# Four plain batches and two seven-product pairs instead of six and one, in a fused attention and FFN kernel

## The chip, the cores and the metric

The kernel runs on one core of a Trainium2 chip. The metric is the device time of one execution in microseconds (us), the median over runs. The core has five engines, each with its own instruction queue that is worked off in order: PE (TensorE, matmuls into eight PSUM banks), DVE (VectorE), ACT (ScalarE), POOL (GpSimd, which has no access to PSUM) and SP (SyncE, which here only issues transfers).

## What is computed

Eight batches; each has 12 heads of 448 positions by 64, so 768 columns. Sigmoid attention, then a mixing of positions by two small matrices, then a feed-forward network (FFN) of width 3072:

```python
scores = scale * np.matmul(q, k.transpose(0, 1, 3, 2)) - np.log(S)
attn = 1.0 / (1.0 + np.exp(-scores))
x = np.matmul(attn, v)            # (8, 12, 448, 64) -> (8, 448, 768)
u = x + (x.transpose(0, 2, 1) @ U @ V).transpose(0, 2, 1)
out = u + np.maximum(u @ w_ch1, 0.0) @ w_ch2
```

## The kernel before

**Numbers in two parts.** Most matmuls are done in 16 bit floats: a 32 bit tile x is scaled and split into a high part (`scaled`, or an ACT instruction) and a rest, x·s minus the high part (`rest`, L329 to L336), and a product takes three matmuls (high·high, high·rest, rest·high). The weights arrive as 64 bit words, are decoded once during batch 0 (`decode`) and are then kept in two parts in memory (`scratch`), from where each later batch fetches them (`fetch`).

**Attention** of a batch is worked through by six head pairs (`pair`). For batches 2 to 7 a head pair loads q, k, v, takes bounds of them on ACT, finds three scales (`scale_by_dma`: a store, a broadcast load and four small DVE instructions), splits q, k and v into one of two staging buffers (STG, POOL and DVE), runs two score operations on PE (each fills four PSUM banks at once), eight sigmoids on ACT, seven splits (POOL for the high part, DVE for the rest) and one value operation on PE. ACT copies its bank into one of six tiles (UB). `mix` then mixes positions, parks the batch's u in memory and, for batches of the plain FFN, splits u into two parts. The UB tiles can be written again when the park has landed.

**The plain FFN** of a batch (`ffn_in`, `ffn_out`) goes by six groups of 512 hidden columns: 4 chains of 18 matmuls in, 6 chains of 12 out, 864 matmuls a batch. After an in chain ACT reads the bank twice (L800, L801) and DVE or POOL makes the rest (L803); after an out chain DVE adds the bank to u.

**The seven-product FFN** takes two batches together: blocks of two by two (two batches, two halves) are multiplied with seven products instead of eight. A pair is 12 in quads (`in_quad`) and 12 out quads (`out_quad`), each 63 matmuls (`product`, L923), in the order iiiiooo iiiooo iiiooo iiooo; a quad takes four of the eight banks. The inputs of the pair are made by `u_forms` (loads of parked u, four subtractions and seven splits for each of three columns). The weights' side needs sums of weight quarters, in two parts: `quarter_sums` copies three quarters, adds and subtracts eight times on POOL and stores four sums through two output buffers (WO, one ACT and one DVE instruction and a store each). There are 24 of them (12 quarters by two weights), and before the change they all run beside attention, in batches 1 to 4 (`FORMS`). `factors` loads a quad's weights into one of four buffers. Tiles of a pair live in any free place of other buffers (`SPOT`; for the making of the inputs `EARLY`, the buffers of attention alone).

**What sets the order.** All operations are first listed with an engine, a planned cost, a position `pos` (a due time) and dependences. `Plan.order` then plays them through: at each moment it takes, among what could start, the operation with the lowest `pos`. The instructions of each engine are emitted in that order, which is fixed from then on. `BEGIN` holds the planned start of each plain batch; the FFN takes its `pos` from it, and attention is spread by a step d per head pair between `BEGIN[1]` and `BEGIN[PLAIN - 1]`. `PLAIN` is the number of plain batches, `LATER` the order in which batches 2 to 7 pass through attention. FFN uses banks `PF` (four), attention `PS_` (four).

## Time and profile before

| | |
|---|---|
| median of 3 runs | 1640.53 us (1640.19 to 1640.63) |
| profiled execution | 1642.12 us, its span 1640.0 us |
| PE, DVE, ACT, POOL busy | 1605.2, 1181.3, 736.5, 616.1 us |
| mean granted TensorE clock | 0.992 |
| moved by DMA | 302.31 MB, 184 GB/s on average |

A span goes from the first to the last instruction of the program; the time of the execution holds a little more around it. Busy times are the union of an engine's instructions. Instructions of one engine can overlap a little, so that the sum of their durations is larger than its busy time; matmuls overlap most, and their cost is read from the distance of their starts.

### The profile page before, as it was taken

What the parts mean: (1) busy time and instruction counts of PE and PEld (TensorE: products, weight loads), DVE (VectorE), ACT (ScalarE), POOL (GpSimd) and SP (SyncE); (2) the same over time, 40 slices, a digit from 0 to 9 for tenths busy, and PEclk for the clock granted to TensorE, in tenths of its full rate; (3) what the DMA queues carried; (4) which work ended last, traced back from release to release, by engine and by line L of the source; (5) the groups of instructions that cost most, each with busy time, mean ns of one, the idle gap of its engine ahead of it and who ended that gap; (6) DMA issues with size and microseconds to landing.
All of it is one profiled execution on the core that took longest, in us unless ns stands there. A gap on an engine that the chain in (4) does not pass through costs nothing.

```text
span 1640.0 us, 24443 instructions
## 1 busy us (share of the span) xinstructions
PE 1605.2 (98%) x8975; PEld 787.5 (48%) x8975; DVE 1181.3 (72%) x2024; ACT 736.5 (45%) x1408; POOL 616.1 (38%) x646
## 2 busy tenths in 40 slices
PE   8989999999999999999999999999999999999999
PEld 3334445544454444445444544544555555555554
DVE  2789999768888788876887787878552357564746
ACT  7566786364545453553555455344311233140310
POOL 0233344447728655843874495257400000000000
PEclk9989999999999999999999999999999999999999
DMA  8757875856666777667765677644783334232331
GB/s 234 256 199 246 310 258 206 285 161 182 198 175 189 209 186 217 167 199 198 228 177 157 199 204 220 173 139 131 185 290 132 119 127 173 104 133 101 118 119 68
DMA packets 203641, 302.31 MB, mean 184 GB/s; under 512 B 106497, under 2 KB 178817, under 8 KB 191233
## 3 DMA queue, kind: packets, MB, share of 16 engines
q1 hardware_dynamic: 203520, 300.75, 59.8%
q8 instruction: 70, 1.15, 0.3%
q14 instruction: 51, 0.41, 0.1%
HBM read 219.81 MB, written 72.60 MB: 178 GB/s over the span
## 4 chain that ended last, share of the span: by engine, by line
PE 73%; DVE 12%; DMA 5%; POOL 5%; issue 2%; ACT 2%; SPq 1%; ACTq 0%; POOLq 0%; DVEq 0%
PE bank L814 22%; PE bank L793 22%; PE bank L923 17%; PE bank L466 4%; PE bank L481 3%; DMA w<-w_in 2%; DVE us__88 L330 2%; POOL w L858 1%; DVE stg__124 L330 1%; PE bank L477 1%; DVE stg__125 L330 1%; POOL w L862 1%; SPq L311 1%; DMA row__136<-far 1%; DMA forms<-xn__121 1%
## 5 line engine op out<-in xcount | busy, mean ns | idle before, releaser
L814 PE MATMUL bank<-h__94,w__92 128*128 128x448 f16 x1296 | 261.6, 354 | 0.0
L814 PE MATMUL bank<-h__93,w__91 128*128 128x448 f16 x1296 | 258.6, 353 | 0.0
L793 PEld LDWEIGHTS <-w__89 128*128 128x128 f16 x1296 | 125.3, 98 | 126.3 <-issue 14.9
L793 PEld LDWEIGHTS <-w__90 128*128 128x128 f16 x1296 | 126.1, 98 | 122.9 <-issue 7.2
L814 PEld LDWEIGHTS <-w__91 128*128 128x128 f16 x1296 | 123.7, 98 | 124.6 <-issue 14.2
L814 PEld LDWEIGHTS <-w__92 128*128 128x128 f16 x1296 | 124.6, 99 | 122.8 <-issue 13.8
L793 PE MATMUL bank<-us__87,w__89 128*128 128x448 f16 x864 | 170.6, 353 | 2.4 <-DVE inv_w__206 L351 1.0
L793 PE MATMUL bank<-us__87,w__90 128*128 128x448 f16 x864 | 172.5, 355 | 0.3 <-POOL w__90 L762 0.3
L862 POOL TENSOR_TENSOR w<-w 128x384 f32<-128x384 f32 x96 | 110.8, 1154 | 3.8
L800 ACT ACTIVATE r__96<-bank 128x448 f32<-128x448 f32 x71 | 38.2, 538 | 146.2 <-PE bank L793 146.2
L800 ACT ACTIVATE r__95<-bank 128x448 f32<-128x448 f32 x73 | 39.4, 540 | 115.5 <-PE bank L793 114.5
L793 PE MATMUL bank<-us__88,w__89 128*128 128x448 f16 x432 | 87.1, 356 | 0.0
L793 PE MATMUL bank<-us__88,w__90 128*128 128x448 f16 x432 | 85.7, 353 | 0.0
L550 ACT ACTIVATE a<-bank,bias_s,c__240 128x448 f32<-128x448 f32 (+1 forms) x96 | 65.6, 723 | 28.7 <-PE bank L466 16.0
L550 ACT ACTIVATE a<-bank,bias_s,c__239 128x448 f32<-128x448 f32 (+1 forms) x96 | 65.8, 723 | 24.7 <-PE bank L466 12.3
L550 ACT ACTIVATE a<-bank,bias_s,c__241 128x448 f32<-128x448 f32 (+1 forms) x96 | 65.4, 721 | 20.2 <-PE bank L466 10.2
L923 PEld LDWEIGHTS <-w__89 128*128 128x128 f16 x441 | 43.1, 98 | 40.3
L803 DVE TENSOR_TENSOR h__94<-r__95,h__94 128x448 f16<-128x448 f32 x36 | 28.6, 796 | 36.0 <-ACT h__94 L801 35.8
L923 PEld LDWEIGHTS <-w__90 128*128 128x128 f16 x378 | 37.0, 98 | 34.5
L923 PEld LDWEIGHTS <-w__91 128*128 128x128 f16 x378 | 37.0, 98 | 34.5
L466 PE MATMUL bank<-stg__124 64*128 64x448 f16 x432 | 48.4, 351 | 2.2 <-ACT a L550 1.9
L466 PE MATMUL bank<-stg__125 64*128 64x448 f16 x432 | 47.7, 351 | 0.2 <-ACT ub__83 L586 0.2
(1164 smaller groups left out, 3263.9 us busy)
## 6 DMA issues: line engine op xcount, KB each, us to landing
w<-w_in SPq DMA_DIRECT2D x48, 768.0 KB, 5.9
w__89<-scratch SPq DMA_DIRECT2D x15, 1536.0 KB, 8.2
w__90<-scratch SPq DMA_DIRECT2D x15, 1536.0 KB, 7.9
w__91<-scratch SPq DMA_DIRECT2D x15, 1536.0 KB, 8.5
w__92<-scratch SPq DMA_DIRECT2D x15, 1536.0 KB, 8.2
w__89<-forms SPq DMA_DIRECT2D x7, 1344.0 KB, 5.7
forms<-xn__120 SPq DMA_DIRECT2D x48, 192.0 KB, 2.9
forms<-xn__121 SPq DMA_DIRECT2D x48, 192.0 KB, 3.3
```

Of the source, the lines that this page charges most:

```text
L311: op("SP", max(0.6, n / 0.30e6), lambda: nc.sync.dma_start(out=dst(), in_=src()), reads, writes, pos, land=land)
L330: nc.vector.scalar_tensor_tensor(out=out, in0=in0, scalar=s, in1=in1, op0=op0, op1=op1)
L466: nc.tensor.matmul(o, keys, y[rows_of(h)], start=i == 0, stop=i == n - 1)
L477: nc.tensor.matmul(av.x[:, :S], x[:, 3, :], y(tiles[3, 0]), start=i == 0, stop=False, skip_group_check=True)
L481: nc.tensor.matmul(av.x[rows_of(h), :S], x[:, j, rows_of(h)], y(tiles[j, h]), start=False, stop=j == 2 and i == n - 1, skip_group_check=True,)
L550: act(0.65 if whole else 0.73, lambda: nc.scalar.activation(out_(), in_(), AF.Sigmoid, bias=bias_s[rows], scale=c if whole else c.x[rows]) ...
L793: nc.tensor.matmul(ph.x[:, :S], wx[:, x, c, f * P : (f + 1) * P], us.x[:, c, y, :], start=c == 0 and i == 0, stop=c == NP - 1 and i == 2,)
L800: act(0.54, lambda: nc.scalar.activation(r.x, ph.x[:, :S], AF.Relu, scale=DOWN_H), [ph], [r], pos - 4)
L803: (pool if on_pool else dve)(1.25 if on_pool else 0.71, lambda: (nc.gpsimd if on_pool else nc.vector).tensor_tensor(out=h.x[:, f, 1, :], i ...
L814: nc.tensor.matmul(po.x[:, :S], wx[:, x, f, e * P : (e + 1) * P], h.x[:, f, y, :], start=f == 0 and i == 0, stop=f == FC - 1 and i == 2,)
L862: pool(0.9, lambda o_=o_, x=x, y=y, sub=sub: nc.gpsimd.tensor_tensor(out=t.x[:, o_], in0=t.x[:, x], in1=t.x[:, y], op=ALU.subtract if sub ...
L923: nc.tensor.matmul(bank.x[:, :S], wt.x[:, k, FACTOR[n], x], both(f)[:, y], start=start and k == i == 0, stop=k == 2 and i == 2, skip_group ...
```

## The change

`PLAIN` falls from 6 to 4, so batches 4 and 5 join 6 and 7 as a second seven-product pair, which runs first. Attention for batches 2 to 7 is now spread to 60 planned us before the end of the last plain batch. From batch 1 on FFN has three banks, and from batch 2 on attention has five. Only weight groups 0 and 1 have their sums made beside plain batches 1 and 2; the other 16 quarter sums read the weights from `scratch` into a buffer of their own (`WSRC`) and stand beside the first pair, which in turn has fewer places for its tiles (`MID`). `u_forms` scales u in place on ACT first, makes its subtractions and two of seven rests on POOL, and for the second pair waits for the last product but seven listed so far (`begun[-8]`, the last of the eleventh in quad). In `scale_by_dma` and `pair` four small DVE instructions become three on POOL. Several planned costs are changed as well.

```diff
-PLAIN = 6
-LATER = [2, 3, 6, 4, 5, 7]
-FORMS = {1: (3,), 2: (1, 4), 3: (2,), 4: (0, 5)}
+PLAIN = 4
+LATER = [2, 4, 3, 5, 6, 7]
+FORMS = {1: (0,), 2: (1,)}
...
+    WSRC = [Buffer(w64h[:, : 24 * P].rearrange("p (x n a b) -> p x n a b", x=2, n=4, a=3))]
...
-    PF, PS_ = BANK[:4], BANK[4:]
+    PF, PS_ = [BANK[:4]] + [BANK[:3]] * (B - 1), [BANK[4:]] * 2 + [BANK[3:]] * (B - 2)
...
+    MID = SPOT[:-10] + SPOT[-6:-4]
...
-        dve(0.17, lambda: ts(nc.vector, inv.x, x(), 2.0 ** -100, ALU.max, 1.0 / TOP, ALU.mult), [e], [inv], pos)
+        pool(0.35, lambda: ts(nc.gpsimd, inv.x, x(), 2.0 ** -100, ALU.max, 1.0 / TOP, ALU.mult), [e], [inv], pos)
         dve(0.17, lambda: nc.vector.reciprocal(out=s.x, in_=inv.x), [inv], [s], pos)
...
-        BEGIN.append(BEGIN[-1] + FFN + (44.0 if not b else 33.0 * len(LATER) / (PLAIN - 2) if b < PLAIN - 1 else 0.0))
+        BEGIN.append(BEGIN[-1] + FFN + (44.0 if not b else 33.0 * len(LATER) / (PLAIN - 1)))
...
-            dve(0.35, lambda: nc.vector.tensor_mul(cc.x, inv.x[:, 0:1], inv.x[:, 1:2]), [inv], [cc], prep + 1)
-            dve(0.15, lambda: ts(nc.vector, cc.x, cc.x, 1.0 / math.sqrt(D), ALU.mult), [cc], [cc], prep + 1)
-            dve(0.15, lambda: ts(nc.vector, cv.x, inv.x[:, 2:3], 1.0 / A_UP, ALU.mult), [inv], [cv], prep + 1)
+            pool(0.35, lambda: ts(nc.gpsimd, cc.x, inv.x[:, 0:1], inv.x[:, 1:2], ALU.mult, 1.0 / math.sqrt(D), ALU.mult), [inv], [cc], prep + 1)
+            pool(0.35, lambda: ts(nc.gpsimd, cv.x, inv.x[:, 2:3], 1.0 / A_UP, ALU.mult, 1.0, ALU.mult), [inv], [cv], prep + 1)
...
-    def quarter_sums(i, b, g, f, pos):
+    def quarter_sums(i, g, f, pos, b=None, after=()):
...
-                load(lambda n_=n_, x=x: far(n_, x), lambda r=r, c=c, x=x: quarter(r, c, x), P * 384 * 2, kw_of(w), [("forms", i, n, n_, x)], pos, 3.0)
+                load(lambda n_=n_, x=x: far(n_, x), lambda r=r, c=c, x=x: cut(far_w, r, c, x), P * 384 * 2, [("scratch", i, g)], [("forms", i, n, n_, x)], pos, 3.0)
...
+        if b is None:
+            w = plan.tile("wsrc", WSRC)
+            for j, (r, c) in enumerate(four_):
+                for x in range(2):
+                    op("SP", 0.7, lambda j=j, r=r, c=c, x=x: nc.sync.dma_start(out=w.x[:, x, j], in_=cut(far_w, r, c, x)),
+                       [("scratch", i, g)], [(w, j, x)], pos - 8, land=2.5, after=after)
...
     def u_forms(b0, b1, pos, after):
...
+            for r, n in ((0, 0), (1, 1), (0, 1), (1, 0)):
+                b, part, t = (b0, b1)[n], c + 3 * r, spot("u", places)
+                op("SP", 0.8, lambda t=t, b=b, part=part: nc.sync.dma_start(out=t.x, in_=parked[b][:, part]),
+                   [("parked", b, part)], [t], at - 3, land=2.5, after=after)
+                act(0.6, lambda t=t: nc.scalar.activation(t.x, t.x, AF.Copy, scale=su.x), [t, su], [t], at)
...
-                dve(0.68, lambda o=o, p_=p_, q_=q_: nc.vector.tensor_tensor(out=o.x, in0=p_.x, in1=q_.x, op=ALU.subtract), [p_, q_], [o], at)
+                pool(1.15, lambda o=o, p_=p_, q_=q_: nc.gpsimd.tensor_tensor(out=o.x, in0=p_.x, in1=q_.x, op=ALU.subtract), [p_, q_], [o], at)
...
-                in_parts(None, su, f, lambda src=src: src.x, [src], at)
+                act(0.57, lambda f=f, src=src: nc.scalar.copy(both(f)[:, 0], src.x), [src], [(f, 0)], at)
+                on_pool = n == 4 or n == 6
+                (pool if on_pool else dve)(1.2 if on_pool else 0.68, lambda f=f, src=src, e=nc.gpsimd if on_pool else nc.vector: e.tensor_tensor(
+                    out=both(f)[:, 1], in0=src.x, in1=both(f)[:, 0], op=ALU.subtract), [src, (f, 0)], [(f, 1)], at)
...
-            d = (BEGIN[PLAIN - 1] - BEGIN[1]) / (NP * len(LATER) + 0.5)
+            d = (BEGIN[PLAIN] - 60.0 - BEGIN[1]) / (NP * len(LATER) + 0.5)
...
-        fs, kg = u_forms(b0, b1, at - 40.0, attended)
+        fs, kg = u_forms(b0, b1, at - 40.0, [values_ops[-1]] if b0 == PLAIN else [begun[-8]])
...
+        if b0 == PLAIN:
+            early = [g for x in FORMS.values() for g in x]
+            for k, n in enumerate(n for n in range(2 * NG) if n // 2 not in early):
+                for i in range(2):
+                    quarter_sums(i, n // 2, n % 2, at - 30 + 20 * k + 10 * i, after=attended)
```

## Rows read from the trace of the kernel before

**Rows 1.** The page's part 1: busy us (share of the span) and instructions of each engine.

```profile
PE 1605.2 (98%) x8975; PEld 787.5 (48%) x8975; DVE 1181.3 (72%) x2024; ACT 736.5 (45%) x1408; POOL 616.1 (38%) x646
```

**Rows 2.** Stretches: length, PE, PEld, DVE, ACT, POOL busy (instructions), clock, DMA share, GB/s.

```profile
410.00:615.00 205.00, 201.19 (x1213) 98.42 (x1209) 166.29 (x285) 105.84 (x212) 126.21 (x140) 0.99 0.70 191
...
1370.00:1490.00 120.00, 120.00 (x636) 62.08 (x635) 74.32 (x124) 31.71 (x58) 0.00 (x0) 1.00 0.37 131
```

**Rows 3.** Timeline of PE: start, length, instruction, out<-in, count.

```profile
1309.42 3.57 PE L793 MATMUL bank<-us__87,w__90 128*128 128x448 f16 x18
1312.82 2.43 PE L814 MATMUL bank<-h__93,w__91 128*128 128x448 f16 x12
...
1338.93 0.73 PE L923 MATMUL bank<-a,w__89 128*128 128x448 f16 x3
...
1374.11 0.73 PE L923 MATMUL bank<-a,w__91 128*128 128x448 f16 x3
...
1386.03 0.73 PE L923 MATMUL bank<-a,w__89 128*128 128x448 f16 x3
```

**Rows 4.** Line 477, first of each value operation: count, ns min/median/max, first and last start.

```profile
L477 PE MATMUL bank<-a__97,stg__124 x54: 352/352/353, 331.9 to 1145.2; 128*128 128x448 f16 x54
...
L477 PE MATMUL bank<-a__104,stg__125 x54: 349/352/353, 348.4 to 1164.9; 128*128 128x448 f16 x54
```

**Rows 5.** Timeline of DVE while the pair's inputs are made.

```profile
1307.99 0.16 DVE L352 RECIPROCAL s_u__259<-inv_u__256 128x1 f32<-128x1 f32 x1
...
1323.83 0.68 DVE L330 SCALAR_TENSOR_TENSOR a__101<-a,s_u__259,a__101 128x448 f16<-128x448 f32 x1
```

**Rows 6.** Timeline of PE: the starts of three successive value operations.

```profile
943.47 0.73 PE L477 MATMUL bank<-a__104,stg__125 128*128 128x448 f16 x3
...
960.02 0.73 PE L477 MATMUL bank<-a__97,stg__124 128*128 128x448 f16 x3
...
978.36 0.73 PE L477 MATMUL bank<-a__104,stg__125 128*128 128x448 f16 x3 [2.78 <-ACT a L550]
```

**Rows 7.** Timeline of POOL; waits from 308 to 1339 (us in total, times, longest).

```profile
945.64 2.07 POOL L327 TENSOR_SCALAR stg__125<-qk__114,s_qkv__236 128x448 f16<-128x448 f32 x2
...
ACT ub__81 L586 <- DMA parked<-ub__81: 11.6, 1, 11.6
```

**Rows 8.** Stretches in which two head pairs pass (columns of rows 2).

```profile
653.00:693.00 40.00, 38.16 (x227) 17.56 (x226) 34.74 (x50) 22.52 (x45) 35.00 (x36) 0.96 0.63 166
...
946.00:981.00 35.00, 32.22 (x207) 15.20 (x206) 30.64 (x46) 19.47 (x37) 32.18 (x33) 1.00 0.71 193
1086.00:1123.00 37.00, 37.00 (x241) 17.70 (x236) 31.17 (x42) 17.91 (x31) 30.41 (x33) 1.00 0.45 134
```

**Rows 9.** From 308 to 1339: all engines; DVE at L867 (sums); L803 (hidden rests).

```profile
308.00:1339.00 1031.00, 1021.59 (x6035) 504.32 (x6034) 754.39 (x1285) 467.20 (x915) 521.28 (x579) 1.00 0.64 184
...
308.00:1339.00 1031.00, 69.29 (x96) 1.00 0.64 184
...
308.00:1339.00 1031.00, 94.00 (x120) 0.00 (x0) 1.00 0.64 184
```

**Rows 10.** Timelines of PE and DVE: an out chain and its addition.

```profile
952.99 2.43 PE L814 MATMUL bank<-h__94,w__92 128*128 128x448 f16 x12
...
959.38 0.67 DVE L330 SCALAR_TENSOR_TENSOR ua__75<-bank,kg__194,ua__75 128x448 f32<-128x448 f32 x1
```

**Rows 11.** Groups of DVE: count | busy us, mean ns | idle before.

```profile
L515 DVE TENSOR_TENSOR c__241<-inv_qkv__235 128x1 f32<-128x1 f32 x12 | 6.4, 530 | 1.0 <-ACT a L550 1.0
```

**Rows 12.** Timeline of POOL: the first additions of three successive quarter sums.

```profile
365.11 0.91 POOL L858 TENSOR_TENSOR w<-w__90 128x384 f32<-128x384 f16 x1 [6.06 <-DMA w__90<-scratch]
...
384.95 4.14 POOL L858 TENSOR_TENSOR w<-w__90 128x384 f32<-128x384 f16 x4 [2.15 <-DVE xn__120 L867]
...
407.99 3.83 POOL L858 TENSOR_TENSOR w<-w__92 128x384 f32<-128x384 f16 x4 [3.49 <-DVE s_qkv__238 L366]
```

**Rows 13.** SP's issues of the parks of tile 86: ns min/median/max, first and last start.

```profile
L311 SPq DMA_DIRECT2D parked<-ub__86 x7: 319/320/628, 293.4 to 1200.7; - x7
```

More of the change, by code (lines that the diff above doesn't have):

```diff
@@ L291, in fused_kernel @@
         spots(x.ap, [x])
-    spots(w64, W64 + XT + WS)
+    for i in range(10):
+        spots(w64[:, i * S // 2 : (i + 1) * S // 2], W64 + (WSRC if i < 4 else []) + (XT[:1] if i < 3 else []) + (XT[1:] if 3 <= i < 6 else []) + (WS if i >= 6 else []))
+    MID = SPOT[:-10] + SPOT[-6:-4]
     WT = []
@@ L449, in scores_of @@
     def scores_of(b, js, products, kp, pos, early):
-        sc = {(j, h): plan.tile("sc", PF + PS_ if early else PS_, False) for j in js for h in range(2)}
+        sc = {(j, h): plan.tile("sc", BANK if early else PS_[b], False) for j in js for h in range(2)}
         n = 1 if b < WHOLE else 3
@@ L579, in pair @@
                     continue
[L580 to L581 removed]
+                pool(0.7, lambda a=a, to=to: scaled(halves(a)[:, 0, :], to.x, A_UP), kto, [(a, 0)], here)
+                dve(0.82, lambda a=a, to=to: rest(halves(a)[:, 1, :], to.x, A_UP, halves(a)[:, 0, :]), kto + [(a, 0)], [(a, 1)], here)
                 keys += [(a, 0), (a, 1)]
@@ L786, in ffn_in @@
         h = hs[b, g]
-        ph = plan.tile("f", PF, False)
+        ph = plan.tile("f", PF[b], False)
         def chain():
@@ L939, in mul @@
         def mul(bank, m, start, pos):
-            product(bank, wt, m, [fs[m, k] for k in range(3)], start, pos, after)
+            begun.append(product(bank, wt, m, [fs[m, k] for k in range(3)], start, pos, after))
         def add(o, bank, y, pos):
```

76 lines of the change are left out of this document (38 added, 38 removed).

## The prediction

> **What bounds the kernel now.** I read the busy times of the page first, then the stages, then single engines. TensorE (PE) is busy 98% of the span [rows 1]. The stages say the same [rows 2]: while attention runs beside the plain feed-forward network (FFN), PE works 201.19 of 205 us with VectorE (DVE) at 166.29 (81%); in the seven-product pair PE works 120.00 of 120 with DVE at 74.32 (62%) and POOL at nothing; the granted clock is 0.99 to 1.00 in both. So PE work that goes is time that goes, as long as the other engines still feed PE.
>
> **The saving.** A plain chain of 18 matmuls starts at 1309.42 and the next chain at 1312.82: 0.189 us a matmul. One quad of 63 in the pair goes from 1374.11 to 1386.03: 11.92 us, again 0.189 each [rows 3]. Two plain batches are 2 x 864 = 1728 matmuls, a pair by seven products 24 x 63 = 1512. The 216 that go are worth 216 x 0.189 = **-40.9 us**, all of it on PE's path. The plain section loses 1728 x 0.189 = 326.7 us, so the first pair, whose first product is now at 1338.93 [rows 3], can start at 1012.2 if PE never starves. The rest of this part is what may starve it.
>
> **Attention for six batches in that time.** The first of the 36 head pairs starts its values at 331.9, the last at 1164.9 [rows 4]: 35 steps of 23.8 us. Before the seven products can start, their inputs are scaled and split: that took from 1307.99 to 1323.83 + 0.68 = 1324.5, so 16.5 us for 21 instructions on ACT and 33 on DVE [rows 5]. The new form has 33 on ACT, so I estimate 16.5 x 33/21 = 26 us, and the last values must start by 1012 - 27 = 985. That leaves (985 - 331.9)/35 = **18.7 us a step**. Can it be held? One step, 960.02 to 978.36, took 18.3 us [rows 6]. The two staging buffers set the floor: one is read by values from 943.47 on, POOL refills it at 945.64, and its next values start at 978.36 [rows 6, 7] and take some 2.5. A life of 35.2 us over two buffers is 17.6 us a step. Between batches comes a further hold: ACT waited 11.6 us for parked data to land before it could empty a bank [rows 7], and a score step takes four banks at once, which is all that attention has. The fifth bank takes one held bank out of the way. So I take the pace as held at 17.6, with a margin of 1.1 us a step.
>
> Is there an engine for it? In three stretches in which two head pairs went by in 35 to 40 us, DVE was busy 84 to 88% and PE 38.16 of 40, 32.22 of 35 and 37.00 of 37 [rows 8]. DVE's work from 308 to 1339 is 754.39 us [rows 9]. From it go two thirds of the sums (69.29 x 2/3 = 46), the rests of two batches' hidden tiles (48 x 94.00/120 = 38), their 72 additions at 0.67 [rows 10] (48), the second scaling of batches 4 and 5 (12 x 0.78 = 9) and the small scale operations of the next paragraph (38): 575 us, in 704 us, or 82%. That is no more than the load of those stretches. PE lost 1.84, 2.78 and 0 us in them, 1.5 per two head pairs or 28 in 36; the whole section lost 1031 - 1021.59 = 9.4 [rows 9]. So the denser attention costs between -9 (nothing is lost any more) and 28 - 9 = 19; I take **+6**, nearer to the section's own rate, which counts every head pair.
>
> **The small scale operations.** Four per head pair, 144 in all, leave DVE, and three come to POOL, as two become one. The largest took 0.53 there [rows 11]; all four are worth between 0.53 and 2.1 us a head pair, 19 to 76 in 36, and I take 38, nearer to the low end, as three of them are single constant scalings. On POOL the trace shows none of this size: 0.53 as on DVE, and 1.04, a quarter of four additions in 4.14 [rows 12], bound it; I take 0.53, 1.6 us a head pair on an engine that loses two thirds of its sums in this section. The new wait is DVE's reciprocal on POOL: it stands behind at most one POOL addition of 1.04, and DVE's next rests stand behind it, so 36 x 1.04 = 37 us of DVE at worst, 87% instead of 82%. PE has FFN chains to run meanwhile; I take 0 of PE's time.
>
> **Banks.** FFN has three instead of four from batch 1 on; a gain is excluded. A chain started at 952.99 and its addition ended at 959.38 + 0.67 = 960.05, so it held its bank for 7.1 us [rows 10]; three out chains last 3 x 2.27 = 6.8. At 0.3 once a head pair the upper end is 11; the lower is 0, since attention's matmuls lie between chains. I take **+2**.
>
> **The sums beside the first pair.** Sixteen of 24 quarter sums move there. Each brings eight additions on POOL, four instructions each on ACT and DVE, four stores, six copies that now read memory, and eight new loads; the 18 issues stand on SP's queue among the factor loads. Additions of successive sums started at 365.11, 384.95 and 407.99 [rows 12]: 19.8 and 23.0 us a sum, with attention's instructions between. Their own part is eight at 1.04 = 8.3 and then two output buffers filled twice; in the pair POOL has nothing else, so I estimate 14.5. SP's issues take 0.32 to 0.63 [rows 13], so 18 are 5.8 to 11.3 and fit. The sums start when the last batch is mixed and parked: 1200.7 - 1164.9 = 36 us after its last values [rows 4, 13], and up to 12 for landing [rows 7]. With the last values at 331.9 + 35 x 17.6 = 948 that is 996. The last sum is wanted before the 22nd of 24 steps, at 1012 + 21 x 11.92 - 6 = 1256: **16.3 us a sum** are there. At 14.5 they are hidden. DVE gets 64 x 0.72 [rows 9] = 46 us more in 286, 62 to 78%. I take **+2** for collisions; the ends are 0 (nothing here is removed from the pair, so no gain) and (19.8 - 16.3) x 16 = 56.
>
> **The second pair's inputs.** Their loads wait for the eleventh of twelve in quads, so four steps, 47.7 us, cover 26 us and some 8 for loads, with fewer free buffers. Uncovered it is 26, covered 0; I take **+4**. The 18 instructions that go to POOL here cost 1.04 x 448/384 = 1.21 each, 22 us, beside ACT's. The Trainium skill (GPSIMD Engine Reference, Engine selection) speaks against this move: elementwise work with two inputs belongs on VectorE, GpSimd being about twice as slow. In this trace it is 1.04 against 69.29/96 = 0.72 for the same 384 elements, 1.4 times [rows 9, 12]; by the page's factor it would be 30 us instead of 22, and the sum some 4 us higher.
>
> **Sum.** -40.9 + 6 + 2 + 2 + 4 = -26.9. The profiled execution took 1642.1 us (its span of 1640.0 and 2.1 around it), 1.6 above the median of the runs: 1642.1 - 26.9 - 1.6 = **1613.6 us**.
>
> **Rivals.** (1) **Attention is late.** The step is 19.2 instead of 17.6, because banks held by values at a change of batch still leave a score step without its four. Then PE stands before the first pair: 0.5 x 35 = 17.5, so 1631. Each further 0.1 costs 3.5, and from 19.4 on nothing is gained. For it: the margin is thin and the mean is 23.8 today. Against: the mean follows the order's own spacing, and the short steps beat 18.7. (2) **The sums set the first pair's length, and the kernel is slower.** The place is its last in quads and last two rounds of out quads, which wait for their factors. From 16.3 us a sum each further us costs 16; from 18.0 on all is lost. At the 19.8 of the rows the time is 1613.6 - 2 + 56 = 1668. For it: no spacing in the rows is under 19. Against: there POOL had attention's work as well. The Trainium skill (SBUF — State Buffer, SBUF: two separate sides) lets a GpSimd instruction and a VectorE one with two SBUF inputs exclude each other, which would push this way; no row here parts that from queueing. (3) **The second pair's inputs lie open**: 1613.6 + 22 = 1636. (4) **All is covered**: 1599.6. That the saving is not there at all I exclude: both pitches are 0.189 at full clock.
>
> **Chances.** The forecast, with (4) in it, 0.66 (1597 to 1627); (1) 0.16; (2) 0.13; (3) 0.05. A measurement of this kernel can tell 0.2%, 3.3 us. Faster: 0.66, and most of (1) and (3), 0.81. Same 0.05; slower 0.14, nearly all of it (2). The range goes from 1597, where nothing starves PE and a little of the -9 comes, to 1645, which takes in (3) and most of (1) and leaves out most of (2).
>
> **What would show it.** Right: 216 fewer FFN and product matmuls at 0.189; the first product at 1012 to 1030; values 17 to 18.5 us apart; no PE gap over 5 us inside the pairs. Wrong: PE idle before the first product, released by ACT, DVE or POOL (1); PE idle in the last third of the first pair, released by a factor load (2); PE idle at the seam of the pairs (3). The forecast falls if values come over 19 us apart or sums over 18.

## The result, and the profile after

The changed kernel takes **1648.16 us** (median of 16 runs, 1643.48 to 1654.15) where the kernel before takes 1641.30 us (16 runs beside it): ratio 1.0042, 95% interval 1.0029 to 1.0054. It is 0.4% slower; 1613.6 us was forecast, with 1597 to 1645 as the range. The profiled execution took 1645.95 us, 2.2 under the median. Executions of these kernels lie some 5 us around their medians, so times below are medians of runs, and single profiles are used for what happens inside them.

The work did go. The page's busy times after, to be held against [rows 1]: 219 fewer matmul records (216 are the change's), DVE 74 us more, POOL 99 us more.

```profile
PE 1576.4 (96%) x8756; PEld 770.4 (47%) x8756; DVE 1255.4 (76%) x2024; ACT 778.7 (47%) x1471; POOL 715.2 (43%) x784
```

The stages after, in the columns of [rows 2]: attention beside plain FFN, three stretches in the first pair, one in the second pair.

```profile
410.00:615.00 205.00, 200.94 (x1260) 96.71 (x1257) 172.93 (x285) 117.95 (x229) 136.14 (x173) 0.99 0.68 194
1400.00:1520.00 120.00, 120.00 (x636) 62.10 (x635) 66.82 (x109) 22.56 (x41) 0.00 (x0) 1.00 0.33 115
1060.00:1160.00 100.00, 100.00 (x531) 51.69 (x530) 81.61 (x125) 36.96 (x71) 57.67 (x52) 1.00 0.79 244
1160.00:1260.00 100.00, 94.40 (x490) 48.09 (x489) 84.89 (x118) 35.30 (x67) 53.38 (x49) 0.98 0.65 193
1260.00:1360.00 100.00, 92.75 (x481) 47.36 (x480) 79.98 (x118) 34.22 (x64) 38.41 (x31) 0.98 0.59 205
```

The second pair is as the one before was, PE at 120.00 of 120 with POOL idle. In the first pair POOL works 38 to 58 us of each 100, DVE rises to 80 to 85, and PE loses 5.6 and 7.3 us in its second and third stretch. None of this is attention: its values, in the columns of [rows 4], go from 331.9 to 972.4, 18.3 us apart, inside the 985 that the prediction asked for.

```profile
L483 PE MATMUL bank<-a__97,stg__124 x54: 349/352/363, 331.9 to 955.0; 128*128 128x448 f16 x54
...
L483 PE MATMUL bank<-a__104,stg__125 x54: 352/352/363, 351.6 to 972.4; 128*128 128x448 f16 x54
```

Yet the first product comes at 1039.29 and not at 1012.2. The timeline of PE ahead of it has the largest hole of the run:

```profile
1011.36 2.43 PE L819 MATMUL bank<-h__93,w__91 128*128 128x448 f16 x12
1026.36 6.28 PE L798 MATMUL bank<-us__87,w__90 128*128 128x448 f16 x18 [12.57 <-DVE ua__77 L336]
1032.48 4.70 PE L819 MATMUL bank<-h__93,w__91 128*128 128x448 f16 x24
...
1039.29 0.73 PE L942 MATMUL bank<-a__98,w__89 128*128 128x448 f16 x3
```

PE waits 12.57 us for a bank, and what frees it is DVE's addition `ua__77`. Why was that late? DVE's timeline shows what stands in front of it, the rests of the first pair's inputs (L929):

```profile
1012.07 0.84 DVE L929 TENSOR_TENSOR a__98<-qk__111,a__98 128x448 f16<-128x448 f32 x1
1012.83 1.55 DVE L929 TENSOR_TENSOR a__99<-qk__112,a__99 128x448 f16<-128x448 f32 x1
...
1024.39 1.32 DVE L929 TENSOR_TENSOR a__109<-a__106,a__109 128x448 f16<-128x448 f32 x1
1025.64 0.67 DVE L336 SCALAR_TENSOR_TENSOR ua__77<-bank,kg__194,ua__77 128x448 f32<-128x448 f32 x1
...
1029.74 0.61 DVE L929 TENSOR_TENSOR qk__113<-a__103,qk__113 128x448 f16<-128x448 f32 x1
```

Ten rests fill 1012.07 to 1025.64, most of them at 1.45 to 1.55 us each; the one at 1029.74, of the same form, takes 0.61, and POOL is idle then. POOL's timeline over the time of the ten has its own subtractions back to back, and they too grew, from 1.14 to 1.5 when DVE's rests began:

```profile
1011.28 1.14 POOL L924 TENSOR_TENSOR a<-qk__113,qk__112 128x448 f32<-128x448 f32 x1
1012.38 1.52 POOL L924 TENSOR_TENSOR a__106<-v__116,qk__113 128x448 f32<-128x448 f32 x1
```

The whole trace says the same. Of the 30 rests L929 that DVE makes for the two pairs, four ran with POOL idle and took 0.61 each; 24 had a two-input instruction of POOL running for at least nine tenths of them and took 0.84 to 1.57.

The hole in PE costs twice. PE's stretches show the granted clock at 0.51, its level of 1.2 GHz, when PE comes back from standing still, and at 1.00 from 1033 on; the first chain took 6.28 us for 18 matmuls that take 3.57 at 2.4 GHz [rows 3].

```profile
1026.00:1032.00 6.00, 5.64 (x16) 0.51 0.00 0
1033.00:1039.00 6.00, 6.00 (x34) 1.00 0.86 269
```

Inside the first pair the waits of PE are of the same kind. They are released by DVE, none by a load of factors:

```profile
PE bank L942 <- DVE ub__84 L336: 4.8, 3, 3.3
PE bank L942 <- DVE ub__85 L336: 3.1, 1, 3.1
PE bank L942 <- DVE v__117 L336: 2.7, 1, 2.7
```

**Theory A** was therefore: two-input work that the change gives to POOL holds DVE up, DVE's bank additions wait behind it, and PE waits for banks. Rivals: three banks (B), the order of the work (D), the sums' transfers (F).

### The profile page after: what moved, and what is told of

Read it like the earlier page. It is cut to its first block, busy times and chain, and to the rows that moved or that the text cites. A ratio compares the mean times of both kernels' runs of the same rounds, so it can differ in the third digit from the quotient of the medians.

```text
span 1644.2 us, 24542 instructions
## 1 busy us (share of the span) xinstructions
PE 1576.4 (96%) x8756; PEld 770.4 (47%) x8756; DVE 1255.4 (76%) x2024; ACT 778.7 (47%) x1471; POOL 715.2 (43%) x784
## 4 chain that ended last, share of the span: by engine, by line
PE 66%; DVE 18%; DMA 6%; POOL 4%; issue 3%; ACT 2%; SPq 0%; ACTq 0%; POOLq 0%; DVEq 0%
PE bank L942 30%; PE bank L819 13%; PE bank L798 11%; PE bank L472 5%; PE bank L487 4%; DVE us__88 L336 2%; PE bank L483 1%; DMA w<-w_in 1%; DVE stg__124 L336 1%; DVE us__87 L336 1%; DVE stg__125 L336 1%; DMA w<-us__88 1%; DVE us__88 L333 1%; DMA parked<-ub__84 1%; PE bank L648 1%
## 5 line engine op out<-in xcount | busy, mean ns | idle before, releaser
L819 PE MATMUL bank<-h__93,w__91 128*128 128x448 f16 x864 | 177.7, 358 | 0.9 <-DVE ua__79 L336 0.9
L819 PE MATMUL bank<-h__94,w__92 128*128 128x448 f16 x864 | 174.6, 355 | 1.5 <-ACT h__93 L806 1.3
L798 PE MATMUL bank<-us__87,w__90 128*128 128x448 f16 x648 | 133.1, 361 | 14.2 <-DVE ua__77 L336 12.6
L798 PE MATMUL bank<-us__87,w__89 128*128 128x448 f16 x648 | 128.9, 355 | 4.1 <-DVE ua__76 L336 2.1
L798 PEld LDWEIGHTS <-w__90 128*128 128x128 f16 x864 | 84.5, 99 | 99.9 <-issue 25.6
L798 PEld LDWEIGHTS <-w__89 128*128 128x128 f16 x864 | 83.9, 99 | 87.4 <-issue 12.9
L819 PEld LDWEIGHTS <-w__91 128*128 128x128 f16 x864 | 82.9, 99 | 88.4 <-issue 19.5
L819 PEld LDWEIGHTS <-w__92 128*128 128x128 f16 x864 | 83.4, 99 | 84.8 <-issue 12.1
L942 PEld LDWEIGHTS <-w__89 128*128 128x128 f16 x819 | 80.7, 99 | 79.2 <-issue 5.6
L877 POOL TENSOR_TENSOR w<-w 128x384 f32<-128x384 f16 x64 | 69.8, 1110 | 103.6 <-DVE xn__120 L886 64.5
L942 PEld LDWEIGHTS <-w__91 128*128 128x128 f16 x756 | 74.2, 98 | 75.7 <-issue 7.5
L942 PEld LDWEIGHTS <-w__90 128*128 128x128 f16 x756 | 74.0, 98 | 70.3 <-issue 1.5
L942 PEld LDWEIGHTS <-w__92 128*128 128x128 f16 x693 | 67.8, 98 | 67.3 <-issue 4.3
L805 ACT ACTIVATE r__96<-bank 128x448 f32<-128x448 f32 x47 | 25.3, 539 | 79.0 <-PE bank L798 79.0
L805 ACT ACTIVATE r__95<-bank 128x448 f32<-128x448 f32 x49 | 26.4, 539 | 57.0 <-PE bank L798 53.3
L885 ACT CAST xn__120<-w 128x384 f16<-128x384 f32 x48 | 24.4, 508 | 51.5 <-DMA forms<-xn__120 24.5
```

The source lines that it names most:

```text
L798: nc.tensor.matmul(ph.x[:, :S], wx[:, x, c, f * P : (f + 1) * P], us.x[:, c, y, :], start=c == 0 and i == 0, stop=c == NP - 1 and i == 2,)
L805: act(0.54, lambda: nc.scalar.activation(r.x, ph.x[:, :S], AF.Relu, scale=DOWN_H), [ph], [r], pos - 4)
L819: nc.tensor.matmul(po.x[:, :S], wx[:, x, f, e * P : (e + 1) * P], h.x[:, f, y, :], start=f == 0 and i == 0, stop=f == FC - 1 and i == 2,)
L877: pool(1.15, lambda j=j: nc.gpsimd.tensor_tensor(out=t.x[:, j], in0=quarter(j, 0), in1=quarter(j, 1), op=ALU.add), [(w, j, 0), (w, j, 1)] ...
L885: act(0.55, lambda o=o, j=j: nc.scalar.copy(o.x[:, :, 0], t.x[:, j]), [(t, j)], [(o, 0)], pos)
L942: nc.tensor.matmul(bank.x[:, :S], wt.x[:, k, FACTOR[n], x], both(f)[:, y], start=start and k == i == 0, stop=k == 2 and i == 2, skip_group ...
```

## The experiments

Times against "the changed kernel" are against its 1648.16 us. Every ratio is against the kernel before, run beside it. The median of that kernel lay between 1641.17 and 1642.44 us, so a difference of a microsecond or two between runs says nothing.

**1. POOL's part of the inputs left out** (`e3_no_u_pool`).

```diff
-            t1, t2, t3, t4 = (spot("ut", places) for _ in range(4))
-            for o, p_, q_ in ((t1, x[0, 1], x[0, 0]), (t3, x[1, 1], x[0, 1]), (t2, x[1, 1], t1), (t4, x[1, 0], t2)):
-                pool(1.15, lambda o=o, p_=p_, q_=q_: nc.gpsimd.tensor_tensor(out=o.x, in0=p_.x, in1=q_.x, op=ALU.subtract), [p_, q_], [o], at)
+            t1, t2, t3, t4 = x[0, 1], x[1, 1], x[1, 1], x[1, 0]
...
+                if on_pool:
+                    act(0.57, lambda f=f, src=src: nc.scalar.copy(both(f)[:, 1], src.x), [src], [(f, 1)], at)
+                    continue
...
```

> Edit: the same 24 subtractions and 12 rests are left out (the copies read a scaled input instead, six rests per pair become copies on ScalarE). Theory A: VectorE's 15 rests for the first pair take 0.61 to 0.68 us each, 10 us in place of 22 us; the idle stretch of 12.57 us falls under 4 us, the first product comes by 1028 us and the time is 1626 to 1634 us. Rival D (the rests are slow for a reason of their own, such as ScalarE beside them, or the stretch waits for the order of VectorE's work): the rests keep 1.3 us or more, or the idle stretch stays over 8 us; time 1642 to 1650 us.

Measured: 1628.34 us, ratio 0.9922 (0.9899 to 0.9945), 19.8 us less. DVE's and PE's timelines, the same places as above:

```profile
1010.72 0.62 DVE L930 TENSOR_TENSOR a__97<-qk__111,a__97 128x448 f16<-128x448 f32 x1
1011.26 0.62 DVE L930 TENSOR_TENSOR a__98<-qk__112,a__98 128x448 f16<-128x448 f32 x1
...
1016.07 0.68 DVE L336 SCALAR_TENSOR_TENSOR ua__77<-bank,kg__194,ua__77 128x448 f32<-128x448 f32 x1
```

```profile
1016.80 6.02 PE L798 MATMUL bank<-us__87,w__90 128*128 128x448 f16 x18 [4.35 <-DVE ua__77 L336]
```

Ten rests now take 1016.07 - 1010.72 = 5.35 us in place of 13.57, which is 8.22 less, and PE's hole shrank by 12.57 - 4.35 = 8.22 in these two profiles. Theory A holds here; 4.35 us of the hole are DVE's order, which has ten rests in front of the addition. The seam of the pairs heals as well: PE is busy 100.00 of 100 us from 1260 to 1360. This run also takes away the subtractions that some rests wait for; the third experiment has no such waits.

**2. The same work given back to DVE** (`e2_u_dve`).

```diff
-                pool(1.15, lambda o=o, p_=p_, q_=q_: nc.gpsimd.tensor_tensor(out=o.x, in0=p_.x, in1=q_.x, op=ALU.subtract), [p_, q_], [o], at)
+                dve(0.68, lambda o=o, p_=p_, q_=q_: nc.vector.tensor_tensor(out=o.x, in0=p_.x, in1=q_.x, op=ALU.subtract), [p_, q_], [o], at)
...
-                on_pool = n == 4 or n == 6
+                on_pool = False
```

> Edit: the 24 subtractions and 12 rests that the changed kernel gives to GpSimd for the two pairs' inputs go back to VectorE. Theory A: the rests take 0.61 to 0.68 us each again, but VectorE has 33 of them for the first pair (about 21 us) in place of 15 at 1.5 us (about 22 us), so the idle stretch in front of the first product stays at 8 to 14 us and the time at 1642 to 1650 us: GpSimd's help was worth nothing. Rival C (the subtractions on GpSimd are a gain, only the order is bad): the time goes up by 8 us or more, to over 1654 us.

Measured: 1645.65 us, 1.0026 (1.0015 to 1.0037), 2.5 less, and the two intervals overlap. POOL's help was worth nothing. DVE's rows say it in one stretch: 0.62 each while POOL is idle, and 1.41 as soon as POOL begins with a sum. PE's hole is now two, of 2.86 and 7.37 us, and both are released by ACT's high part of a hidden tile (L806), not by DVE: with this order another engine is late.

```profile
1010.40 0.62 DVE L924 TENSOR_TENSOR a<-qk__111,a__103 128x448 f32<-128x448 f32 x1
...
1026.84 1.41 DVE L924 TENSOR_TENSOR qk__111<-qk__114 128x448 f32<-128x448 f32 x1
```

**3. The two engines by themselves** (`e7_port`): loops of 16 such instructions.

```diff
...
+            nc.vector.tensor_tensor(out=vo, in0=va, in1=vh, op=ALU.subtract)
...
+            nc.gpsimd.tensor_tensor(out=go, in0=ga, in1=gh, op=ALU.subtract)
...
+            nc.vector.scalar_tensor_tensor(out=vc, in0=bank[:, :S], scalar=2.0, in1=vb, op0=ALU.mult, op1=ALU.add)
...
+            nc.gpsimd.tensor_scalar(out=gc, in0=ga, scalar1=2.0, scalar2=1.0, op0=ALU.mult, op1=ALU.mult)
...
+            nc.vector.tensor_scalar(out=vc, in0=va, scalar1=2.0, scalar2=None, op0=ALU.mult)
...
```

> Nothing of the reference is computed: eight stretches of 16 equal instructions on 128x448 elements, VectorE alone, GpSimd alone, and both together, with one or two inputs in SBUF or one in PSUM. Theory A: a VectorE subtraction of two SBUF inputs takes 0.6 us alone and 1.4 to 1.6 us beside GpSimd subtractions, which go from 1.1 us to 1.4 to 1.6 us; VectorE's addition with one input in PSUM and one in SBUF, and one-input instructions on either side, keep their time alone within 10%. Rival: both keep their times alone in every stretch, and the slow rests come from something else.

The meeting points between the stretches did not keep the engines in step, so a stretch ran beside another than meant; first and last starts tell which. Rows of single lines: ns min/median/max, first and last start.

```profile
L235 DVE TENSOR_TENSOR vo<-va,vh x16: 615/626/626, 5.2 to 15.1; 128x448 f16<-128x448 f32 x16
...
L238 POOL TENSOR_TENSOR go<-ga,gh x16: 1030/1292/1294, 16.0 to 36.3; 128x448 f16<-128x448 f32 x16
...
L241 DVE TENSOR_TENSOR vo<-va,vh x16: 1334/1336/1445, 16.1 to 36.8; 128x448 f16<-128x448 f32 x16
...
L243 POOL TENSOR_TENSOR go<-ga,gh x16: 1027/1032/1034, 38.1 to 54.7; 128x448 f16<-128x448 f32 x16
...
L246 DVE SCALAR_TENSOR_TENSOR vc<-bank,vb x16: 615/624/624, 38.2 to 48.1; 128x448 f32<-128x448 f32 x16
...
L256 POOL TENSOR_SCALAR gc<-ga x16: 559/811/812, 76.0 to 88.0; 128x448 f32<-128x448 f32 x16
...
L259 DVE TENSOR_SCALAR vc<-va x16: 625/1102/1239, 84.2 to 98.1; 128x448 f32<-128x448 f32 x16
```

A DVE subtraction alone takes 0.63 us; beside POOL's (16 to 38 us) DVE does one every 1.38 us, (36.8 - 16.1)/15, and POOL one every 1.35, (36.3 - 16.0)/15. Nothing else runs here and neither waits for the other's results, so ACT, PE, DMA and the order of the work are no causes of it here. Beside DVE's addition with its first input in a bank (38 to 48 us) POOL's subtractions take 1.03, as they do behind it, alone. That addition never ran alone in the loops; it took 0.62 beside POOL here, and in the changed kernel 0.67 both beside POOL (1025.64) and with POOL idle (1031.34). The expectation that one-input instructions go free was wrong: DVE's scaling takes 0.63 beside POOL's scalings and 1.10 beside its subtractions, POOL's scaling 0.56 alone and 0.81 beside DVE's subtractions.

**4. The late sums left out** (`e4_no_late_sums`).

```diff
...
-            for k, n in enumerate(n for n in range(2 * NG) if n // 2 not in early):
+            for n in range(2 * NG):
                 for i in range(2):
-                    quarter_sums(i, n // 2, n % 2, at - 30 + 20 * k + 10 * i, after=attended)
+                    ready[i, n] = ready[i, n % (4 - i)]
```

> Edit: the 16 sums beside the first pair are left out, with their loads, stores and their work on GpSimd, ScalarE and VectorE; quads 4 to 11 read the factors of quads 0 to 3. Theory A (the sums' GpSimd additions slow VectorE beside them): the first pair, 1039.3 to 1354.2 us in the changed kernel (314.9 us), shrinks to 297 to 301 us, and the steps of its quads go back to about 11.9 us; time 1628 to 1634 us. Rival E (three banks or the pair's own VectorE work cause its stalls): the first pair stays over 308 us; time 1641 to 1649 us.

Measured: 1625.94 us, 0.9906 (0.9885 to 0.9928), 22.2 less. PE is busy 100.00 of 100 us from 1160 to 1260 with POOL at nothing; the stretch from 1260 to 1360 still loses 5.0, at the seam. Only part of the gain lies in the pair: in this profile the first product comes at 1027.61, 11.7 us earlier, and the pair then lasts 304.6 us in place of 314.9, where 297 to 301 were expected. The hole before the first product is as long as ever, 12.79. So the sums were taken apart:

**5. Only POOL's additions of the late sums left out** (`e6_no_sum_pool`).

```diff
...
+        if b is not None:
+            for j in range(4):
...
+            y, ky = ((lambda j=j: w.x[:, 0, j]), (w, j, 0)) if b is None else ((lambda j=j: t.x[:, j]), (t, j))
```

> Edit: of the late sums only GpSimd's eight additions each are left out (128 in all); loads, copies on ScalarE, rests on VectorE and stores stay, and read one quarter instead. Theory A: the steps of the first pair from the fourth quad on, 9.0 us over their 11.9 us each in the changed kernel and 8.7 us more around the seam, lose 10 to 17 us of this; time 1630 to 1638 us. Rival (the sums' transfers or their VectorE and ScalarE work cause the stalls): less than 4 us goes; time 1643 to 1650 us.

Measured: 1641.38 us, 1.0001 (0.9987 to 1.0015), 6.8 less: between the two expectations. The stretches from 1160 and from 1260 (columns of [rows 2]) show why: the first is whole, but the seam, where POOL has the second pair's inputs, is as bad as it was.

```profile
1160.00:1260.00 100.00, 100.00 (x531) 51.69 (x530) 68.82 (x130) 36.64 (x71) 0.00 (x0) 1.00 0.68 205
1260.00:1360.00 100.00, 91.13 (x471) 46.56 (x470) 71.83 (x111) 34.23 (x65) 24.39 (x18) 0.97 0.67 225
```

**6 and 7. The sums' transfers from memory to memory.** In the changed kernel all 144 are issued by 485 us, as this row of SP's issues shows (ns, first and last start); only a place in the plan was given to them, and no wait but for their weights.

```profile
L317 SPq DMA_DIRECT2D forms<-scratch x144: 520/625/2102, 85.2 to 485.3; - x144
```

`e5_copies_late` lets 96 of them wait for attention's end, `e9_copies_spread` lets each sum's six wait for a value operation of attention:

```diff
-                load(lambda n_=n_, x=x: far(n_, x), lambda r=r, c=c, x=x: cut(far_w, r, c, x), P * 384 * 2, [("scratch", i, g)], [("forms", i, n, n_, x)], pos, 3.0)
+                op("SP", 0.6, lambda n_=n_, r=r, c=c, x=x: nc.sync.dma_start(out=far(n_, x), in_=cut(far_w, r, c, x)), [("scratch", i, g)], [("forms", i, n, n_, x)], pos, land=3.0, after=after)
```

> Edit: the 96 transfers from memory to memory that copy the late sums' plain quarters wait for the end of attention, as the sums' own loads do; in the changed kernel they went out between 50 and 500 us. Theory F (these transfers, put early into the queue, slow the start and the transposes between 358 and 508 us): the first batch ends about 2 us earlier, TensorE's lost time between 358 and 508 us goes from 8.4 us to under 2 us, and the time is 1636 to 1641 us. Rival (they cost nothing there, or cost the same beside the first pair): 1644 to 1652 us.

Measured: 1708.77 us, 1.0409 (1.0381 to 1.0437), 60.6 more; neither expectation had this. The half of theory F on the early stretch came true: PE is busy 150.00 us of 150 from 358 to 508, and the first product comes at 1031.50, 7.8 us earlier. But then the first pair starves; PE's waits in it, from 1031 to 1300:

```profile
PE bank L942 <- DMA w__90<-forms: 25.5, 3, 16.7
PE bank L942 <- DMA w__92<-forms: 22.0, 3, 12.7
```

The second has `after=gate` in that line, and

```diff
-                    quarter_sums(i, n // 2, n % 2, at - 30 + 20 * k + 10 * i, after=attended)
+                    quarter_sums(i, n // 2, n % 2, at - 30 + 20 * k + 10 * i, after=attended, gate=[values_ops[22 + 2 * k + i]])
```

> Edit: the late sums' 96 transfers from memory to memory go out one sum at a time behind the values of the 23rd to the 53rd head pair in the plan's order (about 520 us to the end of attention), neither between 250 and 500 us as in the changed kernel nor in the first pair as in the run with the copies late. Theory F: TensorE's lost time between 358 and 508 us falls from 8.4 us to under 2 us and nothing starves in the first pair; first product 1030 to 1034 us, time 1638 to 1643 us. Rival (the transfers cost the same wherever attention's own transfers run): the loss moves to 508 to 980 us, time 1645 to 1652 us.

Measured: 1641.60 us, 0.9999 (0.9986 to 1.0012), 6.6 less, as theory F had it. The stretches from 358 to 508 and from 508 to 708, first in the changed kernel and then here: in the first, DMA falls from 0.76 to 0.55 and PE gains 5.3 us; in the second, where the transfers now go, DMA rises from 0.62 to 0.74 and PE loses 3 us more than before.

```profile
358.00:508.00 150.00, 144.71 (x887) 69.08 (x886) 114.07 (x197) 83.34 (x164) 84.36 (x119) 0.99 0.76 215
508.00:708.00 200.00, 191.42 (x1175) 91.50 (x1173) 171.37 (x272) 112.92 (x222) 145.94 (x173) 0.97 0.62 176
```

```profile
358.00:508.00 150.00, 150.00 (x952) 72.64 (x949) 122.86 (x210) 90.02 (x176) 95.72 (x129) 1.00 0.55 165
508.00:708.00 200.00, 188.37 (x1144) 91.15 (x1143) 167.89 (x265) 107.20 (x214) 140.41 (x167) 0.97 0.74 211
```

The first product comes at 1038.38, not at the 1030 to 1034 expected and only 0.9 us before the changed kernel's. So the loss did move in part, as the rival had it, and this profile does not show where the 6.6 us of the medians come from.

**8. Four banks and four** (`e1_banks4`).

```diff
-    PF, PS_ = [BANK[:4]] + [BANK[:3]] * (B - 1), [BANK[4:]] * 2 + [BANK[3:]] * (B - 2)
+    PF, PS_ = [BANK[:4]] * B, [BANK[4:]] * B
```

> Edit: four banks for the FFN and four for attention in every batch, all else as in the changed kernel. Theory A (VectorE and GpSimd hold each other up when both run instructions with two SBUF inputs): the rests of the first pair's inputs still take about 1.5 us each beside GpSimd's subtractions; a fourth bank lets TensorE go on for one more chain, so the idle stretch of 12.57 us shrinks to 7 to 10 us; attention on four banks may cost some of that again; time 1640 to 1650 us. Rival B (three banks are the cause): the idle stretch goes to under 2 us and the half-clock stretch behind it with it; time 1625 to 1632 us, unless the last values come later than 985 us.

Measured: 1709.95 us, 1.0419 (1.0397 to 1.0441), 61.8 more; both theories missed. The values go from 335.0 to 1062.1:

```profile
L483 PE MATMUL bank<-a__97,stg__124 x54: 349/352/581, 335.0 to 1056.9; 128*128 128x448 f16 x54
L483 PE MATMUL bank<-a__104,stg__125 x54: 349/352/577, 356.1 to 1062.1; 128*128 128x448 f16 x54
```

(1062.1 - 335.0)/35 = 20.8 us a step in place of 18.3, so this plan needs attention's fifth bank. Rival B is not decided here: its expectation left out the case of values later than 985. It falls as the whole cause by the last experiment, where FFN has three banks too and PE does not wait in the first pair.

**9. The small operations back on DVE** (`e12_small_dve`): the old four lines of `scale_by_dma` and `pair` in place of the three new ones.

```diff
-        pool(0.35, lambda: ts(nc.gpsimd, inv.x, x(), 2.0 ** -100, ALU.max, 1.0 / TOP, ALU.mult), [e], [inv], pos)
+        dve(0.17, lambda: ts(nc.vector, inv.x, x(), 2.0 ** -100, ALU.max, 1.0 / TOP, ALU.mult), [e], [inv], pos)
...
```

> Edit: the small scale operations of attention go back from GpSimd to VectorE (one more small operation per head pair, on VectorE). Theory: they are worth nothing either way, as predicted: time within 4 us of the changed kernel, 1644 to 1652 us, mean step of the values 18.0 to 18.6 us. Rival H (the one-input operations on GpSimd queue behind its 0.7 us scalings and delay each head pair's scales): the values' mean step falls under 17.9 us and the time by 5 us or more. Rival I (they are a gain, by taking VectorE work away): time over 1653 us.

Measured: 1653.99 us, 1.0076 (1.0049 to 1.0104), 5.8 more, values to 980.4. That is outside the theory's 1652 and in rival I's range, but this interval and the changed kernel's overlap from 1.0049 to 1.0054: the move was a gain of some us, or none; no loss.

**10 to 14. Order alone.** `e8_u_first` gives the first pair's inputs an earlier place, `e10_u_cost` tells the plan the measured 1.5 us, `e11_combo` is `e8_u_first` with `e9_copies_spread`, `e14_all` all three, `e16_seam` lets the second pair's inputs start earlier too.

```diff
-        fs, kg = u_forms(b0, b1, at - 40.0, [values_ops[-1]] if b0 == PLAIN else [begun[-8]])
+        fs, kg = u_forms(b0, b1, at - (110.0 if b0 == PLAIN else 40.0), [values_ops[-1]] if b0 == PLAIN else [begun[-8]])
```

```diff
...
-                (pool if on_pool else dve)(1.2 if on_pool else 0.68, lambda f=f, src=src, e=nc.gpsimd if on_pool else nc.vector: e.tensor_tensor(
+                (pool if on_pool else dve)(1.4 if on_pool else 1.5, lambda f=f, src=src, e=nc.gpsimd if on_pool else nc.vector: e.tensor_tensor(
...
```

> Edit: the first pair's inputs get a place 70 us earlier in the plan, so that they are made as soon as their loads land (about 973 us) and before the last mix, not behind it. Theory A with a missing slack as its second half: the rests are still slow where GpSimd subtracts, but no chain of the last plain batch waits 12.57 us for its bank; the first product comes 10 to 25 us earlier than 1039.3 us, and the time is 1628 to 1642 us. Rival (the bank's wait only moves to another chain, as VectorE has the same work in hand): first product after 1034 us and time 1643 to 1652 us.

> Edit: only the plan's costs of the pairs' inputs change, to what the trace showed beside GpSimd: 1.5 us a subtraction on GpSimd and 1.5 us a rest on VectorE, in place of 1.15 and 0.68 us; the order of the engines' work follows from that. Theory A with the plan as its lever (the order was made for rests of 0.68 us, so TensorE's chains are put too early): the idle stretch of 12.57 us before the first product or the 8.7 us at the seam shrinks by half or more, time 1636 to 1643 us. Rival (VectorE's order around the first pair is forced by what the work needs): both stay, time 1645 to 1651 us.

> Edit: the copies spread over attention and the first pair's inputs 70 us earlier in the plan, both together. If the two costs are apart (about 7 us each by the runs before), the time is 1630 to 1637 us, under the kernel before; if they are the same slack counted twice, it is 1638 to 1645 us.

> Edit: the copies spread, the first pair's inputs 70 us earlier, and the measured costs in the plan of the pairs' inputs, all three. Gains seen singly against the changed kernel: 6.5, 6.6 and 8.9 us, the first two together 9.2 us. If the costs' gain adds to these, 1627 to 1634 us, faster than both kernels; if VectorE's work in the first pair is what is left whatever the order, 1635 to 1642 us.

> Edit: as the run with all three, and the second pair's inputs may start 18 products and 70 us earlier in the plan. If the loss of about 9 us at the seam comes from their VectorE and GpSimd work falling into the last two quads, it shrinks to under 4 us and the time falls by 3 to 8 us; if VectorE is full in the last third of the first pair anyway, the loss only moves forward and the time is within 3 us of the run with all three.

Measured: 1641.54 us (0.9998, 0.9981 to 1.0015); 1639.26 us (0.9986, 0.9970 to 1.0002); 1638.94 us (0.9981, 0.9966 to 0.9995); 1649.05 us (1.0047, 1.0033 to 1.0061); 1648.26 us (1.0047, 1.0029 to 1.0064). Each single order gains 7 to 9 us, `e11_combo` is the one kernel of full work whose interval lies under the kernel before, by 0.2% and as the best of several tried, and all three orders together gain nothing. By their expectations, `e8_u_first` has theory A's time but a first product only 6.6 us earlier where 10 to 25 were expected, `e10_u_cost` is as theory A had it, `e11_combo` shows the same slack counted twice, `e14_all` missed both of its ranges, and `e16_seam` is within 3 us of `e14_all`, as its second half had it. Rival D is right in this much: in `e8_u_first` the one wait of 12.57 us is gone (the waits of PE there are 2.73, 2.41 and 1.14) though POOL does all its work, and the first product comes at 1032.71. In `e14_all` PE stands elsewhere; two of its waits from 960 to 1360, in the columns shown above:

```profile
PE bank L942 <- DVE us__88 L336: 7.0, 1, 7.0
PE bank L819 <- ACT h__93 L806: 4.9, 1, 4.9
```

**15. Half of the late sums back beside plain batches** (`e15_more_early`), on top of `e14_all`, with the values that the transfers wait for set later to suit.

```diff
-FORMS = {1: (0,), 2: (1,)}
+FORMS = {1: (0,), 2: (1,), 3: (2, 3)}
```

> Edit: as the run before it, with two more of the six weight groups summed beside the fourth plain batch, so that 8 sums in place of 16 lie beside the first pair. If the late sums' GpSimd additions are what stalls the first pair (their removal took 9.0 us off quads 10 to 22), its steps go to 11.9 us for most quads and the time is 4 to 8 us under the run before; if the sums only move their cost to attention and the fourth batch's weights, it is the same or up to 15 us slower.

Measured: 1653.65 us, 1.0080 (1.0065 to 1.0095), 4.6 more than `e14_all`. The cost moves with the sums: values end later, at 986, and the first product comes at 1051.

**16. Both parts left out**, as in 1 and 4 (`e13_both_out`).

> Edit: both parts left out together: GpSimd's subtractions and rests for the pairs' inputs, and the 16 late sums. The two runs apart took 19.8 and 22.2 us off the changed kernel's 1648.2 us. If they are two causes that hardly meet, the sum holds: 1604 to 1611 us, which is also where the forecast of 1613.6 us lay, so that nothing large is left to explain. If they share their gain (the same waits of TensorE counted twice), or if a third cost is hidden behind them: 1614 to 1622 us.

Measured: **1614.00 us**, 0.9837 (0.9822 to 0.9851), 34.2 less: the edge of the second range, not the 1604 to 1611 of the plain sum. From 1060 on POOL is empty and PE whole, and of the hole before the first product the share of DVE's order is left:

```profile
1160.00:1260.00 100.00, 100.00 (x530) 51.76 (x529) 55.73 (x92) 17.01 (x31) 0.00 (x0) 1.00 0.32 114
1260.00:1360.00 100.00, 100.00 (x532) 51.87 (x530) 70.73 (x127) 44.62 (x85) 0.00 (x0) 1.00 0.55 195
```

```profile
1013.53 4.96 PE L798 MATMUL bank<-us__87,w__90 128*128 128x448 f16 x18 [4.34 <-DVE ua__77 L336]
```

The two parts were 19.8 and 22.2 alone, 42.0, and 34.2 together: 7.8 us are shared. The miss is 1648.2 - 1613.6 = 34.6 us. The forecast had 2 + 4 for these parts, so they cost 28.2 us more than it said; without them it would have said 1607.6, and the 6.4 us to 1614.0 are other terms' (the wait of 4.34 and the slow chain behind it, 4.96 in place of 3.57, are 5.7 of that size). That 1614.0 lies 0.4 us from the forecast is luck.

## Why the prediction was wrong, step by step

**The step that failed** is the one by which work given to POOL, and the rests behind it on DVE, count as covered: 0 for the first pair's inputs, +2 for the sums, +4 for the second pair's inputs. Together these parts cost 34.2 us. Term by term:

- **The saving** stood: in the second pair PE is busy 120.00 us of 120 at full clock, and with the two parts out the kernel is some 27 us faster than the one before.
- **Attention** stood: the step was 18.3 us, over the 17.6 that the prediction took and under the 18.7 that it allowed, with the last values by 972. Its +6 shows in `e13_both_out`, without the two parts: PE is busy 198.75, 286.67 and 200.00 us of the 200, 300 and 200 from 308 to 1008 and so loses 14.6, against 9.4 before [rows 9]. Rival (1) did not come, and `e1_banks4` shows that it was near: with four banks for attention the step is 20.8 us and the kernel 61.8 us slower.
- **The first pair's inputs** were called covered, at zero, if the last values came by 985. The values came by 972, but the inputs were begun at 1002.85, where the plan's order had put them, and were done at 1034.78 (33.75 + 1.03 on POOL): 32 us for the estimated 26.

```profile
1002.85 1.23 ACT L920 ACTIVATE qk__111<-qk__111,s_u__261 128x448 f32<-128x448 f32 x2
...
1033.75 1.03 POOL L929 TENSOR_TENSOR qk__112<-a__100,qk__112 128x448 f16<-128x448 f32 x1 [4.42 <-ACT qk__112 L927]
```

  Worse, ten of their rests held DVE for 13.57 us and with it a bank: no term stood for what queues behind them on DVE. Leaving POOL's share of both pairs' inputs out gives 19.8 us, with the seam in it.
- **POOL against DVE: the price in it was wrong.** The prediction weighed 1.4 times (the rows) against 2 times (the Trainium skill, GPSIMD Engine Reference, Engine selection). Both leave out the main term: in the lone loops, where the two engines alone differ by 1.03 to 0.63 or 1.6 times, an instruction on POOL makes DVE's beside it last 1.34 instead of 0.63. Moving 36 instructions to POOL bought nothing (`e2_u_dve`).
- **The sums.** The +2 was reasoned by place in the queue: 16.3 us a sum were there, and 14.5 was the estimate. Their first four additions, four a sum, start from 1024.0 to 1276.5, about 16.5 us a sum:

```profile
L877 POOL TENSOR_TENSOR w<-w x64: 899/1221/1760, 1024.0 to 1276.5; 128x384 f32<-128x384 f16 x64
```

  So the estimate was too low. The race was won even so, with the pair itself 27 us late: no wait of the first pair was for factors. Beside it 22.2 us were lost. By the profile without them, 11.7 come before the first product, some 2 of them ahead of 310 us, where profiles differ by as much without any edit there; the six transfers a sum, which the prediction had put beside the first pair, ran up to 485 us against attention's, and the run that holds them back has its first product 7.8 us earlier. 10.3 lie in the pair; without POOL's additions, which stretch DVE's rests, the time is 6.8 us less. These profiles are single ones, and the rest of the sums' cost is not parted.
- **The second pair's inputs**, +4 for being late. They were not late; they held DVE at the seam, as at the start: the longest waits there are the 3.3 and 3.1 us for `ub__84` and `ub__85` shown above, behind rests of 1.45 to 1.56 us, and PE is whole there in `e3_no_u_pool`.
- **Banks**, +2: no run parts their price. With three banks PE had no chain to go on with when one addition was late; what a fourth would have given is open, as the run with four took attention's fifth.
- **Small operations**, 0: back on DVE they are 5.8 us worse, not well parted from none.
- **No term for the clock.** The largest hole of PE cost its length and then most of a chain at 1.2 GHz: 6.28 - 3.57 = 2.7 us, for 15 slow matmuls. Not every wait does: behind the 2.86 us in `e2_u_dve` a chain took its 3.56. In the two profiles 83 matmuls of this size lasted over 0.45 us after and 24 before; at 2.7/15 = 0.18 us each the 59 more are some 11 us, an estimate that lies in the parts above and not beside them.

Rival (2) had the sign and the Trainium skill's rule (SBUF — State Buffer, SBUF: two separate sides) that a GpSimd instruction and a VectorE one with two SBUF inputs shut each other out. I set it aside with "no row here parts that from queueing". That was the wrong call, and a row could: the trace of before has, for single instructions of DVE, not the mean that the prediction used but the spread. These two (ns min/median/max) are a rest of attention and a rest of the sums:

```profile
L330 DVE SCALAR_TENSOR_TENSOR a__108<-a,a__108 x18: 607/968/1352, 341.4 to 1154.2; 128x448 f16<-128x448 f32 x18
```

```profile
L867 DVE TENSOR_TENSOR xn__120<-w,xn__120 x48: 542/628/1360, 373.2 to 1173.9; 128x384 f16<-128x384 f32 x48
```

These are durations, without the time in the queue; one and the same instruction taking 0.61, 0.97 and 1.35 us means that something holds it while it runs. What, the same trace tells: of the rests of sums and hidden tiles from 308 us on (L867, L803), the 93 that ran with POOL idle took 0.54 to 0.63 us, and the 81 that took longer than 0.63 had POOL at work for at least half of their time. Means of 0.72 and 0.78 [rows 9] hid that. The profile of after and the loops agree with the page's rule that the two hold each other up, 1.34 against 0.63; they do not show the second waiting for the whole of the first, as one pair comes every 1.38 us and not every 0.63 + 1.03 = 1.66. For an addition with one input in PSUM they agree that it goes free, 0.62 in the loops and 0.67 in the kernel.

What stays open: why the order edits do not add up (7 us each, nothing in sum); how much of the sums' 22.2 us each of their parts costs; and where the 6.6 us of the spread transfers are gained.

## What to carry to other kernels

Before moving two-input elementwise work from DVE to POOL, count it as time taken from DVE too wherever DVE has work with two SBUF inputs at that moment; in these runs it was free beside DVE additions that read a bank. Look at the spread of one instruction's durations, not only at its mean: it shows held engines before any change is made. And for each stretch of work that is "covered", name the short instruction that frees a bank or buffer behind it in the same engine's queue.
